# A linear-attention and MLP-mixer kernel: hi parts and exponentials on ScalarE, the weights' clamp on GpSimd

## The chip, the cores and the metric

The kernel runs on one core of a Trainium2 chip. Five engines of that core run side by side, each through its own instruction queue in order: TensorE (PE in the profile, with its weight loads as PEld), VectorE (DVE), ScalarE (ACT), GpSimd (POOL) and SyncE (SP, which here only issues DMAs). The metric is the device time of one execution in microseconds. The kernel before took 1183.39 us (median of 3 runs, 1182.16 to 1184.51).

## The reference

```python
def phi(x):                                     # x: q or k, (8, 8, 576, 64)
    proj = einsum('bhsd,df->bhsf', x, w_phi)    # w_phi: (64, 128)
    proj = proj - max(abs(proj), axis=-1, keepdims=True)
    return concatenate([exp(proj), exp(-proj)], axis=-1)
q_p, k_p = phi(q), phi(k)
kv  = einsum('bhsf,bhsd->bhfd', k_p, v);  z = sum(k_p, axis=2)
num = einsum('bhsf,bhfd->bhsd', q_p, kv)
den = einsum('bhsf,bhf->bhs', q_p, z)[..., None] + 1e-6
x   = num / den                                 # as (8, 576, 512)
h   = maximum(x^T @ w_tok1, 0) @ w_tok2         # over the 576 tokens, width 256
u   = x + h^T
out = u + maximum(u @ w_ch1, 0) @ w_ch2         # width 1536
```

The four mixer weights are float64; everything else is float32.

## The kernel before

The work is 32 head pairs of attention (8 batch entries by 4 pairs), 16 token mixings (one for every two pairs), 18 channel mixings (chunks of 256 tokens), and 31 conversions of float64 weights. Most products are made of three float32r products: each operand is split in a high part (the value rounded to float32r) and a low part (the float32 value less its high part), and `mm3` (L62) adds hi·hi, hi·lo and lo·hi. Line 66 therefore carries most of TensorE's work. `split` (L54) makes the two parts; its high part is line 57 on ScalarE or line 59 on another engine, its low part is line 60.

**The streams.** `keys`, `queries`, `token_stream`, `load_weights` and `channel_stream` are generators. `weave` (L532) emits their steps interleaved, by fixed shares and by the steps' yields; after the first token-mixed batch entry the attention streams are emitted with high priority. The tile framework then arranges each engine's order with its own timeline of what every instruction costs. At run time each engine goes through its order and waits for semaphores.

**Attention.** For the first four pairs (`PLAIN`) the projections are single float32 products with 64 contraction rows (L200); for the other 28 pairs, `stack` (L163) puts high and low parts one above the other, so that one product (L196) does both. Its high parts are casts on VectorE (L170), its low parts subtractions on GpSimd (L171). `less_max` (L175) subtracts each row's largest magnitude: a reduction on VectorE (L210), then for stacked pairs a subtraction on GpSimd, for plain keys one on VectorE out of PSUM (both L218), for plain queries a negation on VectorE (L214) and two biased copies on ScalarE (L216). The keys' exponentials (L262) go over two 128-token units in one instruction for each sign; `add_kv` (L284) multiplies them with v. `turn` (L333) transposes query projections into a PSUM tile `pt` (L340) from a group of three banks (`REST`), takes the two exponentials in float32 on ScalarE (`qf`, L347), and splits them: high part `qh` a cast on VectorE (L59), low part `ql` on VectorE for one sign and on GpSimd for the other (L60). `numerators` multiplies with kv (`pn`), and VectorE takes the reciprocal of the denominators (L385).

**Token mixing.** `token_mix` (L399) transposes x in units of 128 rows, one of which has only 64 (the batch entry's last 64 tokens). For it the tile `xs` holds high parts in rows 0-63 and low parts in rows 64-127; two products follow for each of two output halves: `w1_h`, with its 64 rows copied to both halves, by all of `xs` (L416, 128 contraction rows), and the lower 64 rows of `w1_l` by the high parts alone (L418, 64 contraction rows).

**Weights.** `convert` (L99) loads float64 bits, and makes float32 values of them: size of the top word on ScalarE (L116), a clamp on VectorE (L117), three bit operations on VectorE (L118 to L120), then high part on ScalarE (L57) and low part on GpSimd (L60). A channel mixing's `up_proj` and `down_proj` are emitted when their weights' blocks are; the first channel mixing so runs beside the last conversions.

**Start.** GpSimd's queue issues the loads of `w_phi` (L76, L77) and pair 0's v (L253, L255); all other loads are SP's.

Of the kernel before, what the change touches and what calls it, by code (L numbers as in the profile page):

```python
# [8 lines left out]
F32 = mybir.dt.float32  # L9
# [3 lines left out]
AF = mybir.ActivationFunctionType  # L13
ALU = mybir.AluOpType
# [3 lines left out]
P = 128  # L18
B, H, S, D = 8, 8, 576, 64
NP = H // 2              # head pairs  # L20
F = 128                  # random features, before the two signs
C = H * D
T = 256                  # token-mixing width
E = 1536                 # channel-mixing width
NC_, NE, NT = C // P, E // P, T // P
PLAIN = 4                # head pairs at the start, in float32 products: the tensor engine waits then
EARLY = 8                # head pairs for which the scalar engine adds the denominators' 1e-6
BORROWED = 18            # query projections at the start that also use the keys' bank
STAGES = 4               # float64 blocks in flight; their places are the last blocks' of the weights
LAST = 15                # channel-mixing chunk from which the keys' bank serves the chunks too  # L30
LAG = 0.02
CH = 256                 # tokens of a channel-mixing chunk
# Tokens of a batch entry stand as 0-255, 512-575, 256-511, in two tiles:
SEG = [(0, 320), (320, 256)]
# 128-row units of them: (place, rows, first token)
UNITS = [(0, 128, 0), (128, 128, 128), (256, 64, 512), (320, 128, 256), (448, 128, 384)]
# float64 top words, read as float32, between which float32 has the same values
# [4 lines left out]
def mixer_kernel(ctx, tc, qk, vm, vt, w_phi, w1, w2, wc1, wc2d, out):  # L42
    nc = tc.nc
# [10 lines left out]
    def split(hi, lo, raw, eng_hi, eng_lo):  # L54
        """hi + lo is each float32 value of raw exactly."""
        if eng_hi is nc.scalar:
            nc.scalar.copy(hi, raw)  # L57
        else:
            eng_hi.tensor_copy(hi, raw)  # L59
        eng_lo.tensor_tensor(lo, raw, hi.bitcast(F32), op=ALU.subtract)  # L60

    def mm3(o, w, x, first, last, group_ok=False):  # L62
        """o += (w.hi + w.lo)^T (x.hi + x.lo), less the product of the two low parts."""
# [12 lines left out]
    nc.gpsimd.dma_start(wp[D:], w_phi)  # L76
    nc.gpsimd.dma_start(wp[:D], w_phi)  # L77
# [21 lines left out]
    def convert(hi, lo, srcs, name, tag=None):  # L99
        """srcs: float64 bits in DRAM, side by side; hi + lo: their values to float32's 24 bits."""  # L100
# [14 lines left out]
        # the top word's size, held where float32 has exponents for it, then float32's bits of it  # L115
        nc.scalar.activation(m.bitcast(F32), top.bitcast(F32), AF.Abs)  # L116
        nc.vector.tensor_scalar(m.bitcast(F32), m.bitcast(F32), LEAST, MOST, op0=ALU.max, op1=ALU.min)  # L117
# [11 lines left out]
    def load_weights():  # L129
# [6 lines left out]
        nc.scalar.copy(w1_h[D:, 2], w1_h[:D, 2].bitcast(F32))  # L136
# [26 lines left out]
    def stack(raw, base, name):  # L163
        """High and low parts of one of raw's halves, one above the other: head 0; head 1 and both tails."""
        out = []
        lo = D - base
        for k, (c, n) in enumerate(((0, 512), (512, 640))):
            t = wk.tile([P, n], F32R, tag=f"{name[0]}{k}", name=f"st{name}{k}", bufs=1)
            src = raw[base:base + D, c:c + n]
            nc.vector.tensor_copy(t[base:base + D], src)  # L170
# [4 lines left out]
    def less_max(ts, units, name, base=None):  # L175
        """Projections of 128-row units, less each row's largest magnitude; unit (j, u) is head j's
        tokens from 128 u, unit None the last 64 tokens of head 0 and of head 1. ts are stacks, or
        with a base float32 tiles whose rows from there on hold the values."""
# [22 lines left out]
        if base is None:  # L201
# [4 lines left out]
            pr, eng = pr[:, :n], nc.gpsimd  # L206
        else:
            pr, eng = ps[:, :n, 0], nc.vector
        mx = wk.tile([P, 2], F32, tag=f"mx{kind}", name=f"mx{name}")
        nc.vector.tensor_reduce(mx[:, :n], pr, axis=AX.X, op=ALU.max, apply_absolute_value=True)  # L210
        pm = wk.tile([P, 2, F], F32, tag=f"pm{kind}", name=f"pm{name}", bufs=1 if kind == "t" else 2)
        if base == 0:
            nmx = wk.tile([P, 2], F32, tag="nmx", name=f"nmx{name}")
# [381 lines left out]
```

## Time and profile before

| | us |
|---|---|
| median of 3 runs | 1183.39 (1182.16 to 1184.51) |
| profiled execution, first to last instruction | 1182.1 |
| PE busy | 1140.1 (96%), 9032 matmuls |
| PEld busy | 1097.6 (93%) |
| DVE busy | 862.7 (73%) |
| ACT busy | 535.2 (45%) |
| POOL busy | 592.4 (50%) |
| mean granted TensorE clock | 0.991 |

The profiled execution's span lies 1.3 us below the median of the runs, so that the time around the span is no more than the runs' own spread. Busy shares are means over unlike stages: up to about 90 us the plain head pairs and the first 19 weight conversions; up to about 215 us the other 12 conversions beside batch entry 1's attention and the first channel mixing; up to about 1068 us attention, token mixing and channel mixing side by side; then channel mixing alone.

### The profile page before, as it was taken

What the parts mean: (1) busy time and instruction counts of PE and PEld (TensorE: products, weight loads), DVE (VectorE), ACT (ScalarE), POOL (GpSimd) and SP (SyncE); (2) the same over time, 40 slices, a digit from 0 to 9 for tenths busy, and PEclk for the clock granted to TensorE, in tenths of its full rate; (3) what the DMA queues carried; (4) which work ended last, traced back from release to release, by engine and by line L of the source; (5) the groups of instructions that cost most, each with busy time, mean ns of one, the idle gap of its engine ahead of it and who ended that gap; (6) DMA issues with size and microseconds to landing.
All of it is one profiled execution on the core that took longest, in us unless ns stands there. A gap on an engine that the chain in (4) does not pass through costs nothing.

```text
span 1182.1 us, 24091 instructions
## 1 busy us (share of the span) xinstructions
PE 1140.1 (96%) x9032; PEld 1097.6 (93%) x9032; DVE 862.7 (73%) x1782; ACT 535.2 (45%) x1544; POOL 592.4 (50%) x739
## 2 busy tenths in 40 slices
PE   6999978999999999999999999999999999999998
PEld 6778877998999899999999999999999999999998
DVE  7997998868878787877878576684787878663111
ACT  5796655544444445444544353443443445431110
POOL 4345675755555655555646364563564655430000
PEclk9899998999999999999999999999999999999999
DMA  8541131111111011111111011110111110000000
GB/s 228 163 148 31 50 112 44 49 31 49 31 31 49 26 35 40 31 49 31 32 49 31 19 32 49 32 49 10 41 40 40 33 47 12 19 1 19 19 19 19
DMA packets 64149, 54.31 MB, mean 46 GB/s; under 512 B 43617, under 2 KB 55169, under 8 KB 64033
## 3 DMA queue, kind: packets, MB, share of 16 engines
q1 hardware_dynamic: 63824, 52.41, 15.4%
q8 instruction: 72, 1.18, 0.4%
q14 instruction: 45, 0.36, 0.1%
q0 software_dynamic: 208, 0.36, 0.1%
HBM read 43.32 MB, written 9.44 MB: 45 GB/s over the span
## 4 chain that ended last, share of the span: by engine, by line
PE 73%; DVE 15%; ACT 4%; issue 4%; POOL 3%; DMA 0%; SPq 0%; DVEq 0%; ACTq 0%; POOLq 0%
PE h L66 23%; PE acc L66 22%; PE pkv L284 7%; PE pn L66 6%; PE ph L66 4%; PE pa L66 3%; DVE qh L59 2%; PE pt L340 2%; PE ppq L196 2%; PE ppk L196 2%; DVE den L385 2%; DVE ql L60 1%; PE px L407 1%; DVE bitsc L119 1%; DVE bitsc L117 1%
## 5 line engine op out<-in xcount | busy, mean ns | idle before, releaser
L66 PE MATMUL acc<-gh,wc 128*128 128x256 f32 x1728 | 342.0, 283 | 1.5 <-POOL wc L60 1.0
L66 PEld LDWEIGHTS acc<-gh,wc 128*128 128x128 f32 x1728 | 275.3, 189 | 1.9 <-POOL wc L60 1.2
L66 PE MATMUL h<-uh,wc_h 128*128 128x256 f32 x864 | 247.0, 286 | 3.4 <-DVE gl L475 1.8
L66 PE MATMUL h<-uh,wc_l 128*128 128x256 f32 x864 | 246.0, 285 | 0.4 <-POOL wc_l L60 0.4
L66 PE MATMUL h<-ul,wc_h 128*128 128x256 f32 x864 | 245.8, 285 | 0.3 <-POOL ul L455 0.3
L66 PE MATMUL acc<-gl,wc 128*128 128x256 f32 x864 | 241.8, 282 | 1.1 <-DVE gl L475 1.1
L262 ACT ACTIVATE kp<-pmk 128x256 f32<-128x256 f32 (+1 forms) x320 | 109.4, 389 | 164.4 <-POOL pmk L218 156.9
L60 POOL TENSOR_TENSOR ql<-qf,qh 128x320 fp32r<-128x320 f32 (+1 forms) x112 | 104.2, 930 | 133.3 <-DVE qh L59 118.9
L66 PEld LDWEIGHTS h<-uh,wc_h 128*128 128x128 f32 x864 | 163.2, 189 | 5.3 <-DVE gl L475 2.2
L284 PE MATMUL pkv<-v,kp 128*128 128x65 f32 (+1 forms) x1152 | 162.8, 275 | 3.5 <-ACT kp L262 2.5
L66 PEld LDWEIGHTS h<-uh,wc_l 128*128 128x128 f32 x864 | 163.5, 189 | 0.7 <-POOL wc_l L60 0.7
L66 PEld LDWEIGHTS acc<-gl,wc 128*128 128x128 f32 x864 | 162.7, 188 | 1.4 <-DVE gl L475 1.3
L66 PEld LDWEIGHTS h<-ul,wc_h 128*128 128x128 f32 x864 | 163.3, 189 | 0.7 <-POOL ul L455 0.5
L284 PEld LDWEIGHTS pkv<-v,kp 128*128 128x128 f32 x1152 | 153.5, 197 | 8.4 <-ACT kp L262 5.1
L59 DVE CAST qh<-qf 128x320 fp32r<-128x320 f32 (+1 forms) x224 | 110.7, 509 | 43.2 <-ACT qf L347 37.7
L475 DVE SCALAR_TENSOR_TENSOR gl<-h,gh 128x512 fp32r<-128x512 f32 x108 | 73.5, 680 | 90.0 <-ACT gh L474 89.4
L385 DVE RECIPROCAL den<-den 128x320 f32<-128x320 f32 x64 | 124.6, 1947 | 1.6 <-ACT den L381 0.5
L347 ACT ACTIVATE qf<-pt 128x320 f32<-128x320 f32 (+1 forms) x256 | 92.1, 412 | 74.2 <-PE pt L340 69.0
L66 PE MATMUL pn<-qh,kv 128*128 128x320 f32 (+1 forms) x448 | 117.8, 300 | 1.4 <-DVE qh L59 0.7
L474 ACT ACTIVATE gh<-h 128x512 fp32r<-128x512 f32 x108 | 65.0, 602 | 115.2 <-PE h L66 113.2
L386 POOL TENSOR_TENSOR xt<-xt,den 128x320 f32<-128x320 f32 x64 | 53.3, 834 | 113.2 <-DVE den L385 95.7
L455 POOL TENSOR_TENSOR ul<-xt,uh 128x64 fp32r<-128x64 f32 (+3 forms) x120 | 61.5, 536 | 87.1 <-ACT uh L454 86.2
(113 smaller groups left out, 2400.9 us busy)
## 6 DMA issues: line engine op xcount, KB each, us to landing
raw<-in_qk SPq DMA_DIRECT2D x27, 576.0 KB, 3.8
rawc<-in_wc SPq DMA_DIRECT2D x24, 512.0 KB, 4.1
v<-in_vm SPq DMA_DIRECT2D x31, 256.0 KB, 3.4
out_x<-xt SPq DMA_DIRECT2D x12, 256.0 KB, 2.2
out_x<-xt SPq DMA_DIRECT2D x16, 192.0 KB, 2.0
raw<-in_w SPq DMA_DIRECT2D x8, 256.0 KB, 4.4
out_x<-xt SPq DMA_DIRECT2D x16, 128.0 KB, 1.9
pair<-in_qk SPq DMA_DIRECT2D x8, 160.0 KB, 4.6
```

The source lines that it names most:

```text
L59: eng_hi.tensor_copy(hi, raw)
L60: eng_lo.tensor_tensor(lo, raw, hi.bitcast(F32), op=ALU.subtract)
L66: nc.tensor.matmul(o, a, m, start=first and i == 0, stop=last and i == 2, skip_group_check=group_ok)
L196: nc.tensor.matmul(ps[:, i].rearrange("p two f -> p (two f)"), t[:, c:c + P], wp2.rearrange("p two f -> p (two f)"), start=True, stop=True)
L262: nc.scalar.activation(kp[:, :len(us), sg], pm[:, :len(us)], AF.Exp, scale=1.0 - 2.0 * sg)
L284: nc.tensor.matmul(o, kp[:, n, sg], v, start=g == 0 and n == 0 and sg == 0, stop=u is None, skip_group_check=True)
L347: nc.scalar.activation(full, src, AF.Exp, scale=1.0 - 2.0 * sg)
L385: nc.vector.reciprocal(den, den)
L386: nc.gpsimd.tensor_tensor(x, x, den, op=ALU.mult)
L455: nc.gpsimd.tensor_tensor(l[:, d:d + n], t[:, c, o:o + n], h[:, d:d + n].bitcast(F32), op=ALU.subtract)
L474: nc.scalar.activation(gh, ph, AF.Relu)
L475: nc.vector.scalar_tensor_tensor(gl, ph, 0.0, gh.bitcast(F32), op0=ALU.max, op1=ALU.subtract)
```

## The change

Seven edits:

1. `stack`: the high parts of q and k are copies on ScalarE, no longer casts on VectorE.
2. `turn`: the high part of the exponentials is a second exponential on ScalarE straight from PSUM into a float32r tile, no longer a cast on VectorE. The low parts stay where they were.
3. `less_max` for plain pairs: the negated maximum is made on GpSimd, for keys too. For plain keys nothing is subtracted; `keys` takes exp(±proj ∓ max) out of PSUM with the (negated) maximum as the bias, which needs one instruction for each unit and sign (four for a group of two units, before: two).
4. `convert`: the clamp goes to GpSimd (with its two operations in the other order).
5. `token_mix` and `load_weights`: `w1_l`'s 64 rows are copied to rows 64-127 too (one more ScalarE copy at the start), and both products of the 64-row unit use 128 rows of weights and all of `xs`; the product of the two low parts is thereby added.
6. `w_phi` and pair 0's v are loaded from ScalarE's queue instead of GpSimd's.
7. The scratch memory for GpSimd's own DMA descriptors is set to 1024.

```diff
-    nc.gpsimd.dma_start(wp[D:], w_phi)
-    nc.gpsimd.dma_start(wp[:D], w_phi)
+    nc.scalar.dma_start(wp[D:], w_phi)
+    nc.scalar.dma_start(wp[:D], w_phi)
...
-        nc.vector.tensor_scalar(m.bitcast(F32), m.bitcast(F32), LEAST, MOST, op0=ALU.max, op1=ALU.min)
+        nc.gpsimd.tensor_scalar(m.bitcast(F32), m.bitcast(F32), MOST, LEAST, op0=ALU.min, op1=ALU.max)
...
-        nc.scalar.copy(w1_h[D:, 2], w1_h[:D, 2].bitcast(F32))
+        for w in (w1_h, w1_l):
+            nc.scalar.copy(w[D:, 2], w[:D, 2].bitcast(F32))
...
-            nc.vector.tensor_copy(t[base:base + D], src)
+            nc.scalar.copy(t[base:base + D], src)
...
-            pr, eng = pr[:, :n], nc.gpsimd
+            pr = pr[:, :n]
         else:
-            pr, eng = ps[:, :n, 0], nc.vector
+            pr = ps[:, :n, 0]
...
+        if base is not None:
+            nmx = wk.tile([P, 2], F32, tag="nmx", name=f"nmx{name}")
+            nc.gpsimd.tensor_scalar(nmx[:, :n], mx[:, :n], -1.0, None, op0=ALU.mult)
+        if base == D:
+            return pr, nmx, mx
         pm = wk.tile([P, 2, F], F32, tag=f"pm{kind}", name=f"pm{name}", bufs=1 if kind == "t" else 2)
         if base == 0:
-            nmx = wk.tile([P, 2], F32, tag="nmx", name=f"nmx{name}")
-            nc.vector.tensor_scalar(nmx[:, :n], mx[:, :n], -1.0, None, op0=ALU.mult)
             for i in range(n):
                 nc.scalar.activation(pm[:, i], pr[:, i], AF.Identity, bias=nmx[:, i:i + 1])
         else:
-            eng.tensor_tensor(pm[:, :n], pr, mx[:, :n].unsqueeze(2).to_broadcast([P, n, F]), op=ALU.subtract)
+            nc.gpsimd.tensor_tensor(pm[:, :n], pr, mx[:, :n].unsqueeze(2).to_broadcast([P, n, F]), op=ALU.subtract)
...
-            v_sb, queue = vtiles[i % 2], nc.sync if i else nc.gpsimd
+            v_sb, queue = vtiles[i % 2], nc.sync if i else nc.scalar
...
                 for sg in range(2):
-                    nc.scalar.activation(kp[:, :len(us), sg], pm[:, :len(us)], AF.Exp, scale=1.0 - 2.0 * sg)
+                    if i >= PLAIN:
+                        nc.scalar.activation(kp[:, :len(us), sg], pm[:, :len(us)], AF.Exp, scale=1.0 - 2.0 * sg)
+                        continue
+                    for n in range(len(us)):
+                        nc.scalar.activation(kp[:, n, sg], pm[0][:, n], AF.Exp, bias=pm[1 + sg][:, n:n + 1],
+                                             scale=1.0 - 2.0 * sg)
...
-            split(hi, lo, full, nc.vector, nc.gpsimd if sg else nc.vector)
+            nc.scalar.activation(hi, src, AF.Exp, scale=1.0 - 2.0 * sg)
+            (nc.gpsimd if sg else nc.vector).tensor_tensor(lo, full, hi.bitcast(F32), op=ALU.subtract)
...
-                x_all, x_hi = (z.rearrange("p c d -> p (c d)") for z in (xs, xs[:w]))
+                x_all = xs.rearrange("p c d -> p (c d)")
                 for t in range(NT):
                     ts = slice(t * P, (t + 1) * P)
-                    nc.tensor.matmul(pa[:, t], w1_h[:, u, ts], x_all, start=False, stop=False,
-                                     skip_group_check=True)
-                    nc.tensor.matmul(pa[:, t], w1_l[:w, u, ts], x_hi, start=False, stop=False,
-                                     skip_group_check=True)
+                    for w1 in (w1_h, w1_l):
+                        nc.tensor.matmul(pa[:, t], w1[:, u, ts], x_all, start=False, stop=False,
+                                         skip_group_check=True)
...
-    nc = bacc.Bacc("TRN2", target_bir_lowering=False, num_devices=1)
+    nc = bacc.Bacc("TRN2", target_bir_lowering=False, num_devices=1, dynamic_dma_scratch_size=SCRATCH)
```

More of the change, by code (lines that the diff above doesn't have):

```diff
@@ L31 @@
 LAG = 0.02
+SCRATCH = 1024
 CH = 256
```

## The prediction

> **What bounds the kernel now.** I read the page's totals first, then the busy times by stretch, then who made TensorE wait, and last the groups of instructions in those stretches.
>
> ```profile
> span 1182.1 us, 24091 instructions
> ## 1 busy us (share of the span) xinstructions
> PE 1140.1 (96%) x9032; PEld 1097.6 (93%) x9032; DVE 862.7 (73%) x1782; ACT 535.2 (45%) x1544; POOL 592.4 (50%) x739
> ```
>
> TensorE is busy for 96% of the span, so over the whole it is the bound. But the stretches differ (the columns are the stretch, its length, then PE, PEld, DVE, ACT, POOL with their counts, the granted clock and the DMA share):
>
> ```profile
> 0.00:90.00 90.00, 76.32 (x387) 61.64 (x388) 78.64 (x167) 66.44 (x180) 40.86 (x48) 0.94 0.62 177
> 90.00:210.00 120.00, 104.99 (x729) 94.32 (x728) 107.85 (x203) 72.06 (x198) 78.82 (x85) 0.96 0.20 58
> 210.00:1182.00 972.00, 958.77 (x7922) 941.64 (x7920) 676.25 (x1414) 396.69 (x1168) 472.76 (x608) 1.00 0.11 32
> ```
>
> From 210 us on, TensorE does a matmul every 958.77 / 7922 = 0.121 us and idles for 13.2 us of 972: this is a TensorE-bound stage, where only fewer or cheaper matmuls save much. From 90 to 210 us it issues 729; at 0.121 us they are 88.2 us of work, so about 32 us of the 120 are lost, 15.0 as idle time and the rest as matmuls that stand still while they count as busy. VectorE is busy for 107.85 of these 120 us (0.90) and is the bound. Up to 90 us VectorE leads too (78.64 of 90, or 0.87), with ScalarE at 66.44 and 13.7 us of TensorE idle. Who ends TensorE's waits between 90 and 210 us:
>
> ```profile
> PE pn L66 <- DVE ql L60: 2.4, 2, 1.4
> PE ppk L196 <- DVE pk L205: 1.8, 2, 1.3
> PE ph L66 <- DVE al L434: 1.7, 3, 1.2
> ```
>
> The three longest end at VectorE, each at another line: no single wait, but an engine that is late everywhere.
>
> **What VectorE sheds and where it goes.** The groups that the change takes off VectorE, first from 90 to 210 us, then (after the "...") up to 90 us, with the ScalarE groups beside them:
>
> ```profile
> L119 DVE SCALAR_TENSOR_TENSOR bitsc<-rawc,bitsc 128x512 uint32<-128x512 uint32 x12 | 11.4, 958 | 0.0
> L117 DVE TENSOR_SCALAR bitsc<-bitsc 128x512 f32<-128x512 f32 x12 | 8.3, 698 | 0.8 <-ACT bitsc L116 0.8
> L59 DVE CAST qh<-qf 128x320 fp32r<-128x320 f32 x12 | 7.5, 649 | 0.6 <-ACT qf L347 0.5
> L59 DVE CAST qh<-qf 128x256 fp32r<-128x256 f32 x8 | 4.5, 580 | 0.0
> L170 DVE CAST stk<-raw 64x640 fp32r<-64x640 f32 x4 | 2.3, 579 | 0.1
> L170 DVE CAST stk<-raw 64x512 fp32r<-64x512 f32 x4 | 2.1, 530 | 0.2
> L170 DVE CAST stq<-raw 64x640 fp32r<-64x640 f32 x3 | 2.1, 703 | 0.0
> L170 DVE CAST stq<-raw 64x512 fp32r<-64x512 f32 x3 | 1.6, 548 | 0.0
> L214 DVE TENSOR_SCALAR nmxq<-mxq 128x2 f32<-128x2 f32 x2 | 2.7, 1346 | 0.0
> ...
> L262 ACT ACTIVATE kp<-pmk 128x256 f32<-128x256 f32 x32 | 11.7, 415 | 7.3 <-DVE pmk L218 5.9 <-PE pkv L284 1.3
> L216 ACT ACTIVATE pmq<-ppq,nmxq 128x128 f32<-128x128 f32 x28 | 8.6, 360 | 0.7 <-DVE nmxq L214 0.7
> L117 DVE TENSOR_SCALAR bitsc<-bitsc 128x512 f32<-128x512 f32 x12 | 9.2, 769 | 0.0
> L117 DVE TENSOR_SCALAR bits<-bits 128x512 f32<-128x512 f32 x2 | 0.8, 422 | 2.1 <-ACT bits L116 2.1
> L218 DVE TENSOR_TENSOR pmk<-ppk,mxk 128x256 f32<-128x256 f32 x16 | 6.5, 409 | 0.0
> ```
>
> What the same work costs on the other engine, from the whole run's groups (L59 gives the number of casts in all):
>
> ```profile
> L59 DVE CAST qh<-qf 128x256 fp32r<-128x256 f32 x112 | 63.3, 586 | 21.7 <-ACT qf L347 17.5 <-PE pn L66 3.7
> L347 ACT ACTIVATE qf<-pt 128x320 f32<-128x320 f32 x128 | 49.7, 444 | 35.5 <-PE pt L340 35.2
> L59 DVE CAST qh<-qf 128x320 fp32r<-128x320 f32 x112 | 47.4, 432 | 21.4 <-ACT qf L347 20.3
> L347 ACT ACTIVATE qf<-pt 128x256 f32<-128x256 f32 x128 | 42.4, 381 | 38.7 <-PE pt L340 33.8 <-DVE ql L60 1.3 <-DVE stk L170 1.3
> L60 POOL TENSOR_TENSOR wc_l<-bitsc,wc_h 128x512 fp32r<-128x512 f32 x12 | 17.5, 1474 | 10.7 <-ACT wc_h L57 10.5
> L57 ACT CAST wc_h<-bitsc 128x512 fp32r<-128x512 f32 x12 | 7.4, 622 | 3.6 <-DVE bitsc L120 3.5
> masks.py:199 POOL TENSOR_SCALAR_AFFINE_SELECT ident<-ident 128x128 f32<-128x128 f32 x1 | 0.3, 304 | 0.1
> ```
>
> *From 90 to 210 us.* VectorE sheds 12.0 (qh) + 8.1 (stacks' high parts) + 8.3 (clamps) + 2.7 (negations) = 31.1 us and keeps 76.8. ScalarE gains 12 x 0.444 + 8 x 0.381 = 8.4 us of exponentials and 14 copies: a 512-wide cast takes 0.622, a 640-wide one by the slope between 0.381 and 0.444 some 0.75, so 7 x 0.62 + 7 x 0.75 = 9.6. It comes to 72.06 + 18.0 = 90.1. GpSimd gains 12 clamps of a kind that this trace doesn't show: at the least the 0.304 us of its one-input operation on a quarter of the columns, at the most the 1.474 of its two-input operation of the full size. One input is nearer to the first, the size nearer to the second; I take 1.0, so 78.8 + 12.0 = 90.8 (82.5 to 96.5). TensorE's own work is the 88.2. Three engines then stand at 88 to 91; at the 0.90 that VectorE reaches today that is a stretch of 101 us, 19 us less. But a bound shared by three engines in order, with more hand-offs (a conversion now goes ScalarE, GpSimd, VectorE, ScalarE, GpSimd), will not reach 0.90. I take 14 us, from 0 to TensorE's whole loss of 32.
>
> The new waits: VectorE's three bit operations wait for GpSimd's clamp, with evictions such as `gl` and `al` queued behind them, for which TensorE waits; the clamp waits for ScalarE's L116, with the subtractions `pmk` and `pmq` behind it, for which the exponentials and transposes wait.
>
> *Up to 90 us.* VectorE sheds 10.0 us in the rows shown of the clamp, 6.5 of L218's larger form, and its small negations. ScalarE takes over, for each plain group of two key units, four biased exponentials at the 0.360 of L216's biased copies in place of two at 0.415: 64 x 0.360 - 32 x 0.415 = +9.8 us; with the first stacked pair's copies and one `w1_l` copy (about 2.5) it has 78.7. That is what VectorE had (78.64), so one bound takes the other's place: 0, from 6 us better (under half of TensorE's idle time there) to 6 worse. The negations on GpSimd stand in a queue with operations of up to 1.474 us, and the plain keys' two PSUM banks now are held until ScalarE has read them four times: that is the 6 worse. The loads that move to ScalarE's queue cost 0: five issues at 0.6 us (SP issues two in 1.20) lie in the 4.13 us for which ScalarE waits before its first exponential; without that cover some 1.5 us.
>
> ```profile
> 0.75 1.20 SPq L237 DMA_DIRECT2D pair<-in_qk  x2
> ...
> 6.17 1.21 ACT L262 ACTIVATE kp<-pmk 128x256 f32<-128x256 f32 x3 [4.13 <-DVE pmk L218]
> ```
>
> The size of the descriptor scratch is no instruction: 0.
>
> *After 210 us.* VectorE loses 224 - 20 = 204 casts at 0.51 us and 112 - 14 = 98 stack casts at 0.55, and falls from 676 to some 520 of 972 us; ScalarE rises by 204 x 0.41 + 98 x 0.68 = 151 to 548. Neither is a bound. Of TensorE's 13.2 us of idle time I give back 2, from +8 to -10 (below, the fourth rival).
>
> *The 64-row products.* This edit acts on TensorE itself. One token mixing's four products, and what follows them (start, then duration), and the busy time of L418 after 210 us, with its count of 26, two for each token mixing:
>
> ```profile
> 269.40 0.28 PE L416 MATMUL pa<-xs,w_h 128*128 128x256 f32 x1
> 269.61 0.38 PE L418 MATMUL pa<-xs,w_l 64*128 64x256 f32 x1
> 269.92 0.39 PE L416 MATMUL pa<-xs,w_h 128*128 128x256 f32 x1
> 270.24 0.38 PE L418 MATMUL pa<-xs,w_l 64*128 64x256 f32 x1
> 270.55 0.44 PE L407 MATMUL px<-ident,xt 128*128 128x128 f32 x2
> ```
>
> ```profile
> 210.00:1182.00 972.00, 9.89 (x26) 4.75 (x26) 1.00 0.11 32
> ```
>
> From the first start to the next other matmul are 1.15 us; at 0.121 each the four would take 0.48. The steps are 0.21, 0.31, 0.32 and 0.31: products of 128 rows beside those of 64 rows are slow too, not just the small ones. With one shape throughout, 0.67 us go in each token mixing, 13 of which lie after 210 us: 13 x 0.67 = 8.7 us that nothing hides, since TensorE is the bound there. Those before are in the 14 above. (The Trainium skill, TensorEngine Tiling (Array Packing), Key Properties, has it that changing the tiling mode, not merely the tile, drains TensorE. By that rule all four steps shrink, as summed. Were the 64-row shape dear by itself, only L418's two steps would shrink, 13 x 0.38 = 4.9 us, and the sum would end 3.8 us higher. The step of 0.32 after a product of 128 rows speaks for the rule.)
>
> *Sum.* 1182.1 - 14 - 0 - 2 - 8.7 = 1157.4 for the profiled execution. It is 1.3 us below the median of 1183.39, so the median should come to 1158.7.
>
> **The rivals.**
>
> *First: the early gain does not come.* GpSimd's clamps get in VectorE's way. The same 512-wide clamp took 0.422 us for the first two, while GpSimd did little, and 0.698 and 0.769 later; so operations of the two engines hold each other up, and the 12 clamps of 1.0 us may put their 12 us back on VectorE (76.8 + 12 = 88.8). Then four engines stand at 88 to 91 us in chains of five hand-offs, and of the 14 us one is left: 1171.7. Against it: the L59 and L170 casts, which suffer so (0.580 and 0.649 against the 0.432 of the run's mean), are gone from VectorE. (The Trainium skill, SBUF — State Buffer, Who interferes with whom, says that VectorE's casts and tensor_scalar in their fast mode, and its operations with two SBUF inputs, and GpSimd's operations exclude each other for a whole instruction. L119 has two SBUF inputs, and its 0.958 us above agree.)
>
> *Second: the 64-row products stay slow*, because the two output halves or the neighbours in TensorE's order, not the shape, make the steps long. 8.7 us stay: 1167.4. Against it stands that neighbouring `pa` products run at the common pace.
>
> *Third: TensorE is the bound from 90 us on.* All 32 us go, 6 before 90 us, and 8 after 210: 1158.7 - 18 - 6 - 6 = 1128.7. For it: VectorE is the releaser of the longest waits and sheds nearly a third. Against: ScalarE and GpSimd get just what it sheds.
>
> *Fourth, the other side: the queries' chain gets longer.* A piece's four exponentials (4 x 0.41 = 1.65 us, 0.83 before) now stand one after the other on ScalarE before the second sign's low part, they hold `pt`'s bank for that long, and ScalarE's queue also has stack copies of up to 0.75 us and the evictions (`gh`) that TensorE waits for. TensorE's order is fixed, so a late `ql` stops it. After 210 us there are 102 pieces; it decides from 24.7 / 102 = 0.24 us for a piece, and at 0.35 us costs 36 us: 1194.4. For it: ScalarE goes from 397 to 548 us. Against: at 56% it has room, and a cast of 0.43 to 0.59 us leaves the same chain.
>
> **How the numbers follow.** The forecast gets 0.45, the first rival 0.20, the second 0.07, the third 0.13, the fourth 0.15. The range of 1130 to 1186 us leaves out half of the third and most of the fourth. A measurement of this kernel tells about 0.2% (2.4 us) from no change. Faster: the forecast and the first three, 0.85, less 0.05 for mixtures of the first two with a mild fourth that end within 0.2% of before: 0.80. Same: 0.05. Slower: 0.15.
>
> **What would show it.** Right: between 90 and the last conversion, VectorE well below 0.90 and ScalarE and GpSimd at 0.8 or more; the last conversion ending some 15 us earlier than now; the four products of a 64-row unit about 0.12 us apart; after 210 us matmuls no further apart than 0.121 us. Wrong: clamps of over 1.5 us, or L118 to L120 longer than now (first rival); steps of 0.3 us still there (second); waits of TensorE on `qh`, `ql` or `gh` of tens of us in all (fourth); an idle TensorE before 90 us that ends at `kp` on ScalarE by more than 6 us.

## The result, and the profile after

The changed kernel takes 1199.65 us (median of 4 runs, 1194.78 to 1201.9) against 1183.95 for the kernel before beside it: a ratio of 1.0112, with a 95% interval of 1.0081 to 1.0143. It is slower by 1.1%, where 1158.7 us and faster were forecast. The profiled execution took 1199.24 us. One run of this study, of 1198.42 us (edits 5 and 4, below), was a slow one and is left out wherever times are compared at equal clock.

The totals of the page of after:

```profile
span 1197.5 us, 24086 instructions
## 1 busy us (share of the span) xinstructions
PE 1148.0 (96%) x9032; PEld 1110.4 (93%) x9032; DVE 692.5 (58%) x1375; ACT 675.4 (56%) x1913; POOL 604.1 (50%) x805
```

The work moved as the diff says: VectorE lost 170 us, ScalarE gained 140, GpSimd only 12. TensorE issues the same 9032 matmuls and is busy for 8 us longer. The stretches of after, in the prediction's columns (stretch, length, then PE, PEld, DVE, ACT, POOL with counts, granted clock, DMA share and GB/s):

```profile
0.00:90.00 90.00, 76.23 (x305) 60.41 (x305) 59.77 (x96) 65.67 (x184) 59.00 (x92) 0.77 0.63 173
90.00:210.00 120.00, 109.68 (x735) 97.92 (x735) 82.17 (x151) 88.95 (x245) 74.93 (x91) 0.91 0.19 56
210.00:1197.00 987.00, 962.09 (x7996) 952.08 (x7995) 550.53 (x1129) 520.75 (x1486) 470.19 (x623) 0.99 0.11 32
```

In the first 90 us no engine became a new bound: ScalarE, which was to take VectorE's place at 78.7 us, is at 65.67. What differs is that TensorE issued 305 matmuls instead of 387 while being busy as long, and the clock column: 0.77, where it was 0.94. From 90 to 210 us VectorE is well down (0.90 to 0.68), yet the 120 us hold 735 matmuls where they held 729. A finer cut of after shows where the clock went:

```profile
30.00:62.00 32.00, 26.18 (x120) 19.84 (x118) 24.89 (x36) 26.68 (x74) 21.48 (x29) 0.79 0.53 156
62.00:110.00 48.00, 47.47 (x170) 38.07 (x170) 22.49 (x35) 31.11 (x91) 23.40 (x33) 0.50 0.29 89
110.00:210.00 100.00, 89.68 (x666) 82.02 (x666) 76.72 (x143) 79.58 (x217) 71.54 (x83) 0.99 0.21 64
```

From 62 to 110 us TensorE has half its clock throughout (0.50) and is busy for 47.47 of the 48 us. The other engines are busy for 0.47 to 0.65 of it: here TensorE is the bound, at half speed. The like stretch of before had the full clock (1.00) and 267 matmuls:

```profile
58.00:106.00 48.00, 44.68 (x267) 34.55 (x267) 41.97 (x77) 40.56 (x118) 23.60 (x22) 1.00 0.30 91
```

The clock records of the two traces put it exactly: in after one half-speed stretch from 62.2 to 110.0 us (47.8 us) beside shorter ones of 3.4 to 6.8 us; in before only four of 3.4 to 6.8 us. The milestones go with it. Pair 0's attention ends 7.6 us earlier than before (49.5 against 57.1), pair 1's 2.8 later (77.2), pair 2's 22.8 later (111.0 against 88.2). The first product of the first token mixing starts 25 us later (108.5 against 83.4), the last conversion ends 30.9 later (247.3 against 216.4), and the end is 15.4 later (span against span). All of the loss, and more, is there by 111 us.

What stood just ahead of it: TensorE's longest waits up to 90 us, then its order around the start of the slow stretch (start, duration, instruction; in brackets the wait), both of after:

```profile
PE pkv L294 <- ACT kp L271: 5.3, 4, 2.4
PE ppk L202 <- DMA wp<-in_w_phi: 3.8, 1, 3.8
PE pt L350 <- ACT pmq L221: 1.9, 1, 1.9
```

```profile
61.76 2.06 PE L294 MATMUL pkv<-v,kp 128*128 128x65 f32 x8 [2.38 <-ACT kp L271]
84.10 2.50 PE L384 MATMUL pn<-qf,kv 128*128 128x320 f32 x4
```

TensorE stood idle for 2.38 us until 61.8, waiting for a plain key group's exponentials (L271, edit 3's new instructions), and the clock fell at 62.2. ScalarE's queue ahead of them, in after:

```profile
59.95 0.37 ACT L390 COPY xt<-pn 64x256 f32<-64x256 f32 x1
60.33 0.47 ACT L392 ACTIVATE den<-pn,eps 64x256 f32<-64x256 f32 x1
60.82 0.62 ACT L58 CAST wc<-bitsc 128x512 fp32r<-128x512 f32 x1
61.35 0.62 ACT L271 ACTIVATE kp<-ppk,nmxk 128x128 f32<-128x128 f32 x2
```

The exponentials stood behind an eviction, a denominator and a weight's high part, back to back. A gap of 2.4 us is nothing in a sum of waits. So the question for the runs was whether the half clock is the cause, or a companion, of the loss, and what each edit is worth apart from it.

### The profile page after: what moved, and what is told of

It reads as the page before. It is cut to its first block, busy times and chain, and to the rows that moved or that the text cites. A ratio compares the mean times of both kernels' runs of the same rounds, so it can differ in the third digit from the quotient of the medians.

```text
span 1197.5 us, 24086 instructions
## 1 busy us (share of the span) xinstructions
PE 1148.0 (96%) x9032; PEld 1110.4 (93%) x9032; DVE 692.5 (58%) x1375; ACT 675.4 (56%) x1913; POOL 604.1 (50%) x805
## 4 chain that ended last, share of the span: by engine, by line
PE 84%; ACT 7%; DVE 4%; issue 2%; DMA 1%; SPq 0%; POOL 0%; ACTq 0%; DVEq 0%; POOLq 0%
PE h L67 25%; PE acc L67 25%; PE pkv L294 9%; PE pn L67 7%; PE ph L67 3%; PE pt L350 3%; PE pa L67 3%; PE ppk L198 2%; PE ppq L198 2%; PE pn L384 2%; PE px L418 1%; ACT kp L268 1%; ACT qf L357 1%; PE ppq L202 1%; ACT qh L363 1%
## 5 line engine op out<-in xcount | busy, mean ns | idle before, releaser
L67 PE MATMUL acc<-gh,wc 128*128 128x256 f32 x1728 | 337.5, 283 | 3.7 <-ACT gh L484 2.4
L294 PE MATMUL pkv<-v,kp 128*128 128x65 f32 (+1 forms) x1152 | 169.4, 283 | 8.7 <-ACT kp L271 5.3
L294 PEld LDWEIGHTS pkv<-v,kp 128*128 128x128 f32 x1152 | 158.8, 204 | 15.3 <-ACT kp L271 7.4
L364 POOL TENSOR_TENSOR ql<-qf,qh 128x320 fp32r<-128x320 f32 (+1 forms) x112 | 93.6, 836 | 148.2 <-ACT qh L363 147.7
L357 ACT ACTIVATE qf<-pt 128x320 f32<-128x320 f32 (+1 forms) x256 | 104.8, 414 | 88.1 <-PE pt L350 86.8
L268 ACT ACTIVATE kp<-pmk 128x256 f32<-128x256 f32 x280 | 95.9, 391 | 69.3 <-POOL pmk L223 68.6
L364 DVE TENSOR_TENSOR ql<-qf,qh 128x320 fp32r<-128x320 f32 (+1 forms) x112 | 69.6, 622 | 60.2 <-ACT qh L363 59.1
```

Source lines behind the costliest of these rows:

```text
L67: nc.tensor.matmul(o, a, m, start=first and i == 0, stop=last and i == 2, skip_group_check=group_ok)
L268: nc.scalar.activation(kp[:, :len(us), sg], pm[:, :len(us)], AF.Exp, scale=1.0 - 2.0 * sg)
L294: nc.tensor.matmul(o, kp[:, n, sg], v, start=g == 0 and n == 0 and sg == 0, stop=u is None, skip_group_check=True)
L357: nc.scalar.activation(full, src, AF.Exp, scale=1.0 - 2.0 * sg)
L364: (nc.gpsimd if sg else nc.vector).tensor_tensor(lo, full, hi.bitcast(F32), op=ALU.subtract)
```

## The experiments

Every run comes with its mean granted clock (in the records here it is 1.00 or 0.50 of full speed at any moment; the figure is the average over the run), so times can be compared at equal clock. Over 186 runs of the 15 kernels of this study, one line with a common slope and an own level for each kernel gives **0.27 us (± 0.03) of time for each us at half speed** (us at half speed, counted from a clock of 0.99, = (0.99 - clock) x 2 x 1185; residuals of 1.9 us; the ± are two standard errors). The line says that time and clock go together; that the clock is the cause rests on the runs below. "At equal clock" below means a kernel's level on that line less that of before. The clock of before is 0.9888 on average (79 runs, 0.981 to 0.998), that of after 0.9682. On the four occasions of these runs the medians of before were 1185.72 to 1186.31 us; its 1183.95 above is from four runs whose clock is not on record.

### The edits apart

**The 64-row products alone**, edit 5 on the kernel before:

```diff
+        for w in (w1_h, w1_l):
+            nc.scalar.copy(w[D:, 2], w[:D, 2].bitcast(F32))
...
+                    for w1 in (w1_h, w1_l):
+                        nc.tensor.matmul(pa[:, t], w1[:, u, ts], x_all, ...)
```

> The kernel before with edit 5 alone (128 rows of w1_l beside 128 rows of w1_h). The prediction's term: 13 x 0.67 = 8.7 us less, 1174 to 1176 us. Rival, that the saved steps are filled by waits elsewhere: 1180 to 1184 us.

Measured: 1175.9 us, ratio 0.9912 (0.9887 to 0.9937), within the range of the term; at equal clock -8.7 ± 2.0. Its stretches:

```profile
90.00:210.00 120.00, 105.94 (x742) 95.89 (x741) 107.73 (x203) 74.01 (x203) 77.30 (x80) 0.95 0.19 58
210.00:1176.00 966.00, 950.99 (x7934) 940.97 (x7933) 679.66 (x1420) 398.58 (x1174) 475.97 (x614) 1.00 0.11 33
```

TensorE's busy time after 210 us falls from 958.77 to 950.99 with 12 matmuls more in it. This edit does what its term said; it is also the fastest kernel of the study, faster than both kernels of the case.

**The plain keys' exponentials alone** (edit 3 on the kernel before), and **the whole change without them**:

```diff
+        if base == D:
+            return pr, nmx, mx
...
+                        nc.scalar.activation(kp[:, n, sg], pm[0][:, n], AF.Exp, bias=pm[1 + sg][:, n:n + 1],
+                                             scale=1.0 - 2.0 * sg)
```

> The kernel before with edit 3 alone. If edit 3 is what loses the clock: mean clock 0.965 to 0.975 and 1198 to 1208 us. If it needs the other edits: 1178 to 1188 us with a clock of 0.985 or more. If ScalarE's added 10 us are the price without any clock: 1188 to 1195 us at 0.985 or more.

> The changed kernel with edit 3 undone (plain pairs' subtraction and negation on VectorE again, two exponentials a group). Clock theory, with the gap before kp as its start: no half clock from 62 to 110 us, mean clock 0.985 or more, 1168 to 1182 us. Rival, that any new order loses the clock: clock about 0.97, 1190 to 1205 us. Rival (steady): 1195 or more with a clock of 0.985.

Measured: alone 1191.9 us, ratio 1.0045 (1.0022 to 1.0069), at equal clock +4.5 ± 1.3, with a clock of 0.982 to 0.991: the third of the three cases, a price of its own. Alone it doesn't lose the long stretch (the longest half-speed stretches of its trace are two of 13.7 us). After without it: 1186.89 us, ratio 1.0008 (0.9996 to 1.002), with the clock back at 0.983 to 0.991, as the clock theory had it, though the time lies 5 us above its range. Undoing this one edit gives back 12.8 us, and at equal clock it gives nothing that can be told (-1.0 ± 1.3 without it, -0.5 ± 2.5 with it). So in the whole change edit 3 costs by the clock.

**The 64-row products with the clamp** (edits 5 and 4), and **with the high parts** (edits 5, 1 and 2):

```diff
-        nc.vector.tensor_scalar(m.bitcast(F32), m.bitcast(F32), LEAST, MOST, op0=ALU.max, op1=ALU.min)
+        nc.gpsimd.tensor_scalar(m.bitcast(F32), m.bitcast(F32), MOST, LEAST, op0=ALU.min, op1=ALU.max)
```

```diff
-            nc.vector.tensor_copy(t[base:base + D], src)
+            nc.scalar.copy(t[base:base + D], src)
...
-            split(hi, lo, full, nc.vector, nc.gpsimd if sg else nc.vector)
+            nc.scalar.activation(hi, src, AF.Exp, scale=1.0 - 2.0 * sg)
+            (nc.gpsimd if sg else nc.vector).tensor_tensor(lo, full, hi.bitcast(F32), op=ALU.subtract)
```

> The kernel before with edits 5 and 4 (128-row w1_l, clamp on GpSimd). Edit 5 alone took 1175.9 us. If the clamp's move is what makes the run without edit 3 no faster than before: 1182 to 1188 us, with the last conversion 5 to 14 us later than in the run of edit 5 alone. If it is the high parts: 1174 to 1178 us. The prediction's theory (VectorE bounds 90 to 210 us): 1170 to 1174 us.

> The kernel before with edits 5, 1 and 2 (128-row w1_l, high parts and float32r exponentials on ScalarE). If the high parts' move is what costs: 1182 to 1188 us. If it is the clamp: 1172 to 1178 us. The prediction's theory (VectorE bounds 90 to 210 us): 1160 to 1170 us.

Measured: with the clamp 1184.11 us, ratio 0.9985 (0.9956 to 1.0013), at equal clock -4.2 ± 1.4; with the high parts 1180.88, ratio 0.9949 (0.9903 to 0.9996), at equal clock -6.6 ± 1.8. Beside the -8.7 of edit 5 alone, the clamp costs 4.5 ± 2.3 and the high parts 2.1 ± 2.6: the first loses, as its case expected, and for the second neither a gain nor a loss can be told. Its median lies between its two cases, and its level hangs on one of its five runs: 1191.13 us at a clock of 0.987 is some 10 us off the line, and without that run the high parts come to -0.5 ± 2.5. The 1160 to 1170 us of the theory that VectorE is the bound are missed either way. The kernel with the high parts from 90 to 210 us:

```profile
90.00:210.00 120.00, 105.32 (x726) 96.54 (x725) 94.94 (x170) 88.43 (x240) 74.75 (x80) 0.92 0.19 58
```

VectorE falls from 107.73 us (edit 5 alone, above) to 94.94, and the matmuls in the stretch go from 742 to 726. From the end of the 20th conversion to the end of the 31st it takes 63.3 us with edit 5 alone, 65.0 here, 66.3 in before and 73.1 in after. Lightening VectorE by a tenth did not shorten what it was said to bound.

### The clock

**Bursts of extra products between the plain projections.** They read `wp2` and write a bank that the next projection overwrites. First five short ones, then a single long one:

```diff
+        if name in FED:               # five names in the first kernel, one in the second
+            for _ in range(12):       # 28 in the second
+                nc.tensor.matmul(ps[:, 0].rearrange("p two f -> p (two f)"), wp2[:, 0],
+                                 wp2.rearrange("p two f -> p (two f)"), start=True, stop=True)
```

> The changed kernel with 60 more float32r products of 256 columns, whose results are overwritten, in five bursts of 12 among the plain keys' projections of pairs 1 to 3 (4 x 512 more columns in all are no part of the result). Theory (clock): TensorE lost some 20 us between 60 and 110 us because it ran there at half the clock while it was busy; the bursts bring the clock back, the mean clock comes to 0.985 or more and the time to 1176 to 1187 us. Rival (queues): ScalarE's and GpSimd's queues set the pace there, the clock only follows; the bursts change nothing or cost 6 to 13 us: 1199 to 1213 us. Rival (steady): the loss is in the queries' chain after 210 us: 1199 or more.

> The changed kernel with 28 float32r products of 256 columns, whose results are overwritten, before one projection of pair 2's keys (about 62 us; that work is no part of the result). 28 products fill a whole 3.4 us window of the clock at half speed wherever it begins. Clock theory: half speed from 62 us ends within about 7 us of the burst; TensorE gains up to 20 us until 110 us, less 3 to 6 for the burst: 1180 to 1188 us at a clock of 0.98 or more. Rival (queues): 1200 to 1206 us.

Measured: five short bursts 1192.97 us, ratio 1.0056 (1.0026 to 1.0086); one long burst 1199.65, ratio 1.0087 (1.0057 to 1.0117). Neither median is in the clock theory's range. Both hide two groups of runs of the same program, and the clock tells them apart:

| | runs | clock | us |
|---|---|---|---|
| five bursts of 12 | 4 | 0.986 to 0.990 | 1188.8 to 1190.8 |
| | 4 | 0.980 to 0.981 | 1195.2 to 1196.5 |
| one burst of 28 | 4 | 0.979 to 0.984 | 1191.0 to 1192.8 |
| | 6 | 0.969 to 0.973 | 1199.6 to 1204.3 |

The code is the same within a kernel, so no order or hand-off of the program differs: the time goes with the clock. But whether a burst brings the clock back was a matter of the run, which the theory had not allowed for. Even in the trace of the single burst, of a run of the faster group, half speed comes again at 65.3 us, for 23.9 us. The kernels couldn't be called a cure.

**Only two plain pairs** (`PLAIN = 2`), so that stacked products, which have 128 rows, come sooner:

```diff
-PLAIN = 4
+PLAIN = 2
```

> The changed kernel with two plain head pairs, not four, so that pairs 2 and 3 use float32r stacks. Clock theory: from 60 us on enough dense products keep or bring back the full clock; clock 0.985 or more and 1172 to 1186 us. Rival (queues): more stacks and subtractions for ScalarE and GpSimd early on; 1195 to 1210 us.

Measured: 1212.1 us, ratio 1.0198 (1.0158 to 1.0238), with a clock of 0.960 to 0.969. The expectation failed. Its trace lost the clock earlier, from 40.4 to 88.2 us, and there TensorE is not even busy all the time:

```profile
40.00:90.00 50.00, 38.54 (x134) 30.04 (x135) 42.58 (x54) 32.45 (x84) 35.60 (x38) 0.52 0.38 119
```

At equal clock it is still 10.1 ± 2.6 slower than before: stacked pairs that early cost by themselves. This run tells nothing for the clock's rule but that having fewer plain pairs is no way around it.

**What counts as busy.** A reading of the traces: in their first 130 us, cut in the 3.41 us steps in which the clock record changes, I added up for every step the columns that TensorE's matmul instructions moved, times two for float32 and one for float32r, times rows/128. At half speed, every step of 3,160 or more was followed by full speed, and none of 3,050 or less; at full speed, every step of 2,920 or less was followed by half speed and none of 3,250 or more. All 15 traces of this study fit. Both weights are needed: without the one for rows, slow steps of up to 4,250 stayed slow while some of 3,160 ended the slow stretch; without the one for float32 it is 2,590 against 1,530.

The amount, some 3,100, is about the same in both directions, but a step holds less at half speed: at the pace of after 210 us (256 columns every 0.121 us) a fast step holds 7,200, and 28 products of 256 columns that follow each other at half speed (22 of them in 5.06 us, below) come to 3,800 a step before the weight for rows. So 3,100 are some 43% of a fast step and 82% of a slow one, and such a clock sticks.

In after, the step with the gap of 2.38 us (58.8 to 62.2 us) holds 1,495; the 13 slow steps that follow hold 1,770 to 2,980, and the one that ends the slow stretch 4,070. From the timeline above, eight instructions of 65 columns in 2.06 us are 8 x 65 x 2 / 2.06 x 3.41 = 1,720 a step, without any pause between them. The 320-column products at 84.10 come to 4 x 320 x 2 / 2.50 x 3.41 = 3,490, but for 2.5 us only. And the plain projections have 64 rows, so they count for half.

This makes a prediction that rows alone can test: beside three bursts of 28 products over 128 rows, which had run before this reading, the same three over 64 rows.

```diff
+        if name in FED:               # k2_0, k2_2, k3_0
+            for _ in range(28):
+                nc.tensor.matmul(ps[:, 0].rearrange("p two f -> p (two f)"), wp2[:, 0], ...)
...
+                nc.tensor.matmul(ps[:, 0].rearrange("p two f -> p (two f)"), wp2[D:, 0], ...)
```

> The changed kernel with three bursts of 28 float32r products, whose results are overwritten, before projections of the keys of pair 2 (two) and of pair 3 (one). One burst gave a clock of 0.979 to 0.984 and 1191 to 1193 us in four of ten runs, 0.969 to 0.973 and 1200 to 1204 in six. Clock theory: with three, nearly all runs have 0.979 or more and 1188 to 1198 us, in spite of some 10 to 15 us of added products. Rival (queues): 1205 to 1215 us, whatever the clock.

> The run with three bursts again, with 64 contraction rows in the bursts' products in place of 128: as many products of as many columns, for the same time, whose results are overwritten. In the traces so far a 3.41 us window of the clock at half speed is followed by full speed only if its products fill about 3,100 column steps or more (a column of float32r one step, of float32 two, both weighted by the share of the 128 rows used), of 4096. If rows count so, 28 products of 64 rows bring no window there: clock 0.96 to 0.975 and 1199 to 1210 us. Rival, that TensorE's being busy is what counts: as with 128 rows, clock 0.986 to 0.990 and 1190 to 1194 us.

Measured: 128 rows 1191.97 us, ratio 1.0056 (1.0038 to 1.0074), clock 0.986 to 0.990 in all ten runs; 64 rows 1198.5 us, ratio 1.0103 (1.0073 to 1.0134), clock 0.976 to 0.980 in all five, a little better than the 0.96 to 0.975 and 1199 to 1210 us expected if rows count, and far from the 0.986 to 0.990 of the rival. The stretch from 60 to 110 us, first with 128 rows, then with 64, and one of the 64-row bursts:

```profile
60.00:110.00 50.00, 44.03 (x260) 36.34 (x259) 30.40 (x44) 38.38 (x112) 25.97 (x39) 0.87 0.33 99
```

```profile
60.00:110.00 50.00, 48.14 (x217) 38.52 (x217) 23.00 (x34) 30.22 (x89) 20.31 (x33) 0.62 0.27 85
...
57.21 5.06 PE L198 MATMUL ppk<-wp 64*128 64x256 f32 x22
```

The 64-row burst filled 5 us without a gap, and the clock did not rise: its trace reads half speed for 44.4 us from 53.3 on. By the count, 22 x 256 / 2 / 5.06 x 3.41 = 1,900 a step; over 128 rows the same would be 3,800. At equal clock the two kernels are alike (+5.6 ± 1.3 and +5.6 ± 1.9, so the bursts themselves cost about 6 us beside after's -0.5), and the 6.5 us between them are the clock's: (0.9884 - 0.9784) x 2 x 1185 x 0.27 = 6.4. The 64-row kernel's clock is still above after's 0.968, so its bursts did something, but they did not end the stretch. What ends it is neither the lack of pauses nor the number of products and their columns, which are the same in both; the rows that they fill decide. (The Trainium skill, TensorE: Matmul & The Clock Gate, Part 1: The HAM clock gate, says that the full clock follows one busy window of about 3.4 us, and gives no measure of busy. The steps of 3.41 us agree; a TensorE busy for 47.47 of 48 us at 0.50 does not, if busy is read as the profile reads it. The same part also warns that the clock's trace events can be unreliable; here the times of 186 runs follow them, with residuals of 1.9 us.)

### The buffers of ScalarE's and GpSimd's hand-offs

A theory for the flat stage from 90 to 210 us was that the four places shared by the conversions' words and the channel mixing's evictions (tag "g") hold it up. Eight places, with edits 5 to 7; then with edits 1 and 2 too; then on the whole change:

```diff
-        m = wk.tile([P, 512], U32, tag="g", name=f"bits{name}", bufs=4)[:w, :n]
+        m = wk.tile([P, 512], U32, tag="g", name=f"bits{name}", bufs=8)[:w, :n]
...
-            gh = wk.tile([P, 2, CH], F32R, tag="g", name=f"gh{i}_{ep}", bufs=4)
-            gl = wk.tile([P, 2, CH], F32R, tag="g", name=f"gl{i}_{ep}", bufs=4)
+            gh = wk.tile([P, 2, CH], F32R, tag="g", name=f"gh{i}_{ep}", bufs=8)
+            gl = wk.tile([P, 2, CH], F32R, tag="g", name=f"gl{i}_{ep}", bufs=8)
```

> The kernel before with edits 5, 6 and 7 and eight places, not four, in the group that conversions (bits) and channel mixing (gh, gl) share. Edit 5 alone took 1175.9 us. Theory (places): the conversions after 140 us come at 5 to 6 us apart with VectorE loaded or not, because they wait for places and for each other; with eight places the last conversion ends 5 to 20 us earlier and the time is 1160 to 1172 us. Rival (order): their pace is the order in which they are emitted and loaded; no change, 1173 to 1179 us.

> The kernel of the run before this one, and edits 1 and 2 (high parts and float32r exponentials on ScalarE). If VectorE bounds 90 to 210 us once places don't: 5 to 15 us less than that run. If VectorE is no bound there: within 4 us of it.

> The changed kernel with eight places in that group. Theory (places): the 24 us by which the last conversion is late shrink by 5 to 20, and the time by as much: 1180 to 1195 us at the same clock of about 0.97. Rival (order): 1196 to 1203 us.

Measured: 1186.51 us, 1.0009 (0.9979 to 1.0038); 1183.45, 0.9973 (0.9942 to 1.0004); 1193.15, 1.0054 (1.0028 to 1.008). At equal clock -7.8 ± 1.6, -10.3 ± 1.5 and -2.1 ± 1.8: against the same edits with four places the differences are +0.9 ± 2.5, -3.6 ± 2.1 (-1.1 ± 2.1 without the outlying run named above) and -1.6 ± 2.5. With eight places, the high parts are worth -2.4 ± 1.8: within the 4 us that stood for VectorE being no bound. The 1193.15 us lie in the range of the theory of places, but by luck: most of what they are below after's time is the clock's (0.975 on average, against 0.968). Places and high parts together shorten the time from the end of the 20th conversion to that of the 31st to 52.9 us, where the places alone leave 67.0 and the high parts alone 65.0:

```profile
90.00:210.00 120.00, 102.74 (x739) 94.22 (x738) 94.55 (x173) 89.82 (x243) 75.23 (x82) 0.96 0.22 65
```

But VectorE, ScalarE and the count of matmuls stand there as they did without the places, and the end moves by at most 3.6 us of the 12. In the whole change the places shorten it from 73.1 to 55.9 us, and the end moves by 1.6 ± 2.5. The conversions weren't what the end waited for. Two more things count. The first of these kernels has no edit 3 and lost the clock all the same (0.970 to 0.981; half speed for 27.3 us from 39.9 and for 20.5 from 70.6). It takes 10.6 us more than edit 5 alone, which neither of its two cases allowed for, and all of it goes with the clock; so edit 3 is one trigger and not the only one. Whether edit 6, edit 7 or the places lost it there was not tested; after without edit 3 has edits 6 and 7 and kept its clock. And one run of the second kernel at 0.991 took 1172.44 us, the lowest time of the study.

## Why the prediction was wrong

**The loss is the clock's.** After runs at 0.9682, before at 0.9888: (0.9888 - 0.9682) x 2 x 1185 = 48.8 us more at half speed, by 0.27 that is 13.2 us, and at equal clock nothing that can be told is left (-0.5 ± 2.5). (2.0 of the 15.7 us come of the four runs of before, whose median is 1183.95 where that of its 79 later runs is 1185.94.) The runs bear it out: undoing edit 3 brings the clock and 12.8 us back, two kernels split into two times by the clock alone, and bursts that differ only in rows differ in clock and time.

**The step that failed first is "up to 90 us: 0, from 6 us better to 6 worse".** It weighed VectorE against ScalarE by their sums. Those sums were fair: 72 biased exponentials took 0.381 and 0.370 us where 0.360 was taken. The 6 worse named the right place, GpSimd's negations and ScalarE's queue, and TensorE did wait 5.3 us for `kp`, inside the 6 that were to mark it wrong. But the price of that wait was taken as its own length. In a stage whose products use half the rows or 65 columns, the clock fell right behind one gap of 2.38 us, and for 47.8 us no step of that stage was dense enough to win it back. That the gap took it is read from one trace and the count above; that edit 3 did is shown by undoing it. The prediction showed the clock column, 0.94 up to 90 us, and gave it no term. It lacked the question: what does the clock do if TensorE stops here?

**The step that failed next is "VectorE is the bound" from 90 to 210 us, worth 14.** The engine's shift came as forecast, or cheaper:

```profile
L363 ACT ACTIVATE qh<-pt 128x320 fp32r<-128x320 f32 x112 | 50.1, 447 | 0.0
L363 ACT ACTIVATE qh<-pt 128x256 fp32r<-128x256 f32 x112 | 43.5, 388 | 0.4
L172 ACT CAST stq<-raw 64x640 fp32r<-64x640 f32 x28 | 20.5, 732 | 0.3
L118 POOL TENSOR_SCALAR bitsc<-bitsc 128x512 f32<-128x512 f32 x24 | 17.5, 729 | 3.8 <-ACT bitsc L117 3.2
L172 ACT CAST stk<-raw 64x512 fp32r<-64x512 f32 x28 | 17.3, 617 | 3.9 <-PE ppk L198 2.6 <-DMA raw<-in_qk 0.7
L271 ACT ACTIVATE kp<-ppk,mxk 128x128 f32<-128x128 f32 x36 | 11.7, 381 | 0.0
L271 ACT ACTIVATE kp<-ppk,nmxk 128x128 f32<-128x128 f32 x36 | 11.6, 370 | 5.1 <-POOL nmxk L215 5.1
```

These whole-run groups of after (count | busy us, mean ns | idle time before them) stand beside 0.444 and 0.381 for the exponentials, 0.75 and 0.62 for the copies, and 1.0 for GpSimd's clamp. So the prices were right and their use was not. That an engine is busy for 0.90 of a stretch and ends the longest waits did not make it the bound: those waits were 1.2 to 1.4 us each at the longest, and taking a tenth off VectorE gained nothing with four places and 2.4 ± 1.8 us with eight, far from 14. What sets the pace of that stage at equal clock **stays open**. At that size the runs exclude VectorE's load alone, the four places alone, and the conversions' pace as the thing the end waits for.

**The first rival was right that the clamp brings no gain; its mechanism is only in part borne out.** The clamp on GpSimd costs 4.5 ± 2.3 us, where the rival let the early gain of 14 shrink to 1. Its mark, longer bit operations on VectorE, came. Two of them in before from 90 to 210 us, then (after the "...") all three in after, with GpSimd's clamp:

```profile
L120 DVE SCALAR_TENSOR_TENSOR bitsc<-rawc,bitsc 128x512 uint32<-128x512 uint32 x11 | 7.9, 720 | 0.0
L118 DVE TENSOR_SCALAR bitsc<-bitsc 128x512 uint32<-128x512 uint32 x12 | 7.2, 604 | 0.1
...
L121 DVE SCALAR_TENSOR_TENSOR bitsc<-rawc,bitsc 128x512 uint32<-128x512 uint32 x8 | 9.1, 1143 | 0.2
L120 DVE SCALAR_TENSOR_TENSOR bitsc<-rawc,bitsc 128x512 uint32<-128x512 uint32 x8 | 7.8, 970 | 0.1
L119 DVE TENSOR_SCALAR bitsc<-bitsc 128x512 uint32<-128x512 uint32 x8 | 6.9, 858 | 1.7 <-POOL bitsc L118 1.7
L118 POOL TENSOR_SCALAR bitsc<-bitsc 128x512 f32<-128x512 f32 x8 | 5.6, 710 | 0.1
```

L121 and L119 take 1.143 and 0.858 us where the same operations of before (its L120 and L118) took 0.720 and 0.604 in that stretch; L120 (before: L119) stays at 0.97. There the clamp saves VectorE 0.70 us a conversion and 0.68 come back. But the stretch holds 8 conversions of after and 12 of before. Over the 24 conversions of this size in the whole run the three operations go from 2.27 to 2.58 us: of the 0.73 that the clamp took, 0.31 come back, and VectorE is still relieved. So this doesn't account for the 4.5 us, and what the clamp's move costs stays open. The case against the rival had a slip, too: it set the 0.580 us of the 128x256 casts beside the 0.432 of the 128x320 ones; the 128x256 casts take 0.586 on average, so only the 0.649 showed a delay. (The Trainium skill, SBUF — State Buffer, Who interferes with whom, has a VectorE operation with two SBUF inputs and a GpSimd operation that reads SBUF contend for a shared port; the longer L121 agrees with it, while L120, also with two inputs, stays at 0.97.)

**The 64-row products were right**: -8.7 was the term, -8.7 ± 2.0 the run. The second rival falls. In after, a unit's four products:

```profile
292.83 0.28 PE L428 MATMUL pa<-xs,w_h 128*128 128x256 f32 x1
292.94 0.28 PE L428 MATMUL pa<-xs,w_l 128*128 128x256 f32 x1
293.06 0.28 PE L428 MATMUL pa<-xs,w_h 128*128 128x256 f32 x1
293.18 0.28 PE L428 MATMUL pa<-xs,w_l 128*128 128x256 f32 x1
293.30 0.38 PE L418 MATMUL px<-ident,xt 128*128 128x128 f32 x2
```

They start 0.11 to 0.12 us apart, where the steps were 0.21 to 0.32.

**Edits 6 and 7, costed at nothing,** had no run of their own. With eight places beside edit 5 they came to +0.9 ± 2.5 at equal clock, which doesn't contradict it; but that kernel lost the clock, and whether they had a part in it is not known.

**The third rival** wanted all of TensorE's loss back; none came. **The fourth**, the queries' longer chain, forecast 1194.4 us, near the measured time, for a reason that isn't so. TensorE's waits on `qh`, `ql` and `gh`, which were to be tens of us, come to 5.9 us in after, and the chunks of the channel mixing are 22 us late by the middle of the kernel and 15.6 at the end, so after 210 us the kernel gains on the one before. A time that fits is no evidence for its mechanism.

At equal clock the parts add up within their errors: -8.7 (products) + 4.5 (plain keys) + 2.1 (high parts) + 4.5 (clamp) = +2.4, against -0.5 ± 2.5 for the whole, each part with 1.3 to 2.6 of its own. Only one of the four gained that can be told.

## What to carry to other kernels

Read the clock column before the busy columns, and ask of every edit near a stage of sparse products (few rows, or few columns by the count above) what one more gap does to the clock there. When a stage has three engines at 0.9, unloading one of them is a guess until a kernel with that one edit has run. Time the parts of a compound change apart: here one of the seven edits alone made the kernel 0.9% faster than before, and the others took that back and more.

## What the runs showed of the hardware that was not expected

- **A TensorE without a pause can stay at half speed.** It did for 47.8 us at 47.47 of 48 busy. What brings the clock back depends on the rows that the products fill: three bursts of 28 products over 128 rows did it in every run (0.986 to 0.990), the same over 64 rows in none (0.976 to 0.980). The figure of some 3,100 column steps in 3.41 us is an inference from the counts in 15 traces; only its dependence on rows was tested by a run.
- **A us at half speed costs 0.27 us in this kernel**, not 0.5 or 1. Why was not tested; after makes up some of the delay later (its channel mixing is 22 us late at first and 15.6 at the end).
- **More than half of the unchanged kernel's spread goes with the clock.** Before took 1180 to 1194 us in 79 runs, with clocks from 0.998 to 0.981; the clock accounts for 58% of the variance.
